# Attention forward and backward: all transposes of the probability and score-gradient slabs through the DMA crossbar, none on TensorE

## The chip, the cores and the metric

The kernel runs on one core of a Trainium2 chip. The time is device microseconds of that core, median over executions. A gain is told as a ratio: the mean time of one kernel's fast runs over the mean of the other kernel's fast runs of the same rounds on the same chip, so it is not quite the ratio of the medians that are quoted.

Engine names are those of the profile: PE is TensorE (PEld its weight loads), DVE is VectorE, ACT is ScalarE, POOL is GpSimd, SP is SyncE, whose queue issues the DMA transposes. L458 is line 458 of the kernel before; the changed kernel has the same line numbers.

## The reference, cut to what matters

The reference computes a block and all its gradients. Only the attention part is touched by the change:

```python
def _A_ref(x, k_cache, v_cache, wq, wo):
    B, Sq, D = x.shape            # 1, 2048, 576
    H, Dh = 32, 128               # 32 heads of 128; 2048 keys
    q = (x @ wq).reshape(B, Sq, H, Dh).transpose(0, 2, 1, 3)
    scores = einsum("bhqd,bhkd->bhqk", q, k_cache) * (Dh ** -0.5)
    p = softmax(scores, axis=-1)
    o = einsum("bhqk,bhkd->bhqd", p, v_cache)
    return o.transpose(0, 2, 1, 3).reshape(B, Sq, H * Dh) @ wo
# ... the whole: x + s * silu(gated MLP); outputs: the result and vjp gradients
```

For a head, the backward pass needs dV = P^T dO, dP = dO V^T, dS = P * (dP - delta), dQ = dS K and dK = dS^T Q. P and dS are 2048 x 2048 a head. They are held as 16 "slabs" of 128 rows. O = P V and dQ = dS K need each slab transposed: the kernel hands the transposed tile to these matmuls as `lhsT`.

## The kernel before: the parts that matter

A head has two phases. Phase 1 makes the scores, softmax, P slabs, O and half of dV. Phase 2 makes dP, dS slabs (written over the P slabs), dQ, the rest of dV and half of dK. The other half of dK comes in the next head's phase 1. Each slab is transposed in one of two ways:

```python
pe_p = set(cfg.get("pe_p", [0, 1, 3, 4, 6, 7, 9, 10, 12, 13, 15]))   # P slabs on TensorE: 11 of 16
pe_ds = set(cfg.get("pe_ds", [2, 5, 8, 11, 14]))                     # dS slabs on TensorE: 5 of 16
dma_p = lambda qt: qt not in pe_p
dma_ds = lambda qt: qt not in pe_ds
# ...
def transpose_slab(hs, qt, use_dma, name, engs):
    Pq = hs.slabs[qt]
    T = wpt.tile([P, NT, P], bf, name=name, tag="PT")        # 9 buffers
    if use_dma:
        nc.sync.dma_start_transpose(T[:], Pq[:])             # L452, SP queue
    else:
        for gi, g in enumerate(range(0, NT, 8)):             # the kernel's n = min(8, NT - g) is written as 8
            pt = acc_tile(bf)                                # PSUM
            for j in range(8):
                nc.tensor.transpose(pt[:, j, :], Pq[:, (g + j) * P:(g + j + 1) * P], ident[:])   # L458
            alt.copy(T[:, g:g + 8, :], pt[:, :8, :], eng=engs[gi % len(engs)])                  # L40/L42
    return T
```

A schedule gives each slab a "main" step (scores or dP and their elementwise work), a "trans" step and a "tail" step. The tail is the 16 matmuls that read the transposed slab: L500 for O, L539 for dQ. A DMA transpose is issued at the main step and used five steps later. A TensorE transpose is issued one step after main and used one step later still:

```python
SKEW_DMA = cfg.get("skew_dma", 5)
SKEW_PE = cfg.get("skew_pe", 1)
PE_TSKEW = cfg.get("pe_tskew", 1)
t_tr = qt + (0 if d else PE_TSKEW)
t_tail = t_tr + (SKEW_DMA if d else SKEW_PE)
```

## Time and profile before

| | before |
|---|---|
| time, median of 2 | 6170.7 us |
| attention stage | about 825 to 4552 us |
| head period (mean, from the second head on) | 116.3 us |
| phase 1 / phase 2 | 63.4 / 53.0 us |
| moved by DMA, a head | 12.8 MB, 110 GB/s |

The head period and the phases are differences of start times in the trace: the first weight load of a head's scores (L470) and of its dP (L523).

First the windows view. Each line is a stretch, its length, the busy time of the engines (with instructions), the granted TensorE clock, the DMA share and GB/s. The first line is the whole attention stage; the next two are phase 1 and phase 2 of one typical head.

```profile
825.00:4552.00 3727.00, 3509.97 (x46957) 2849.17 (x46955) 3144.78 (x6748) 2572.65 (x4256) 767.03 (x1305) 1.00 0.58 109
...
3609.30:3672.70 63.40, 61.66 (x845) 50.90 (x845) 56.50 (x146) 46.38 (x87) 12.78 (x26) 1.00 0.40 91
3672.70:3725.60 52.90, 48.11 (x631) 38.27 (x629) 41.87 (x68) 33.81 (x47) 11.41 (x15) 1.00 0.72 134
```

PE is busy 94% of the stage, DVE 84%, ACT 69%. Phase 1 is the fuller one on PE and the emptier one on DMA (0.40). It has 11 of its slabs on TensorE.

"Busy" overstates a pipelined engine. From start to start, a 128-column matmul takes 56 ns and a 512-column one 215 ns, while one lasts 219 and 377 ns. Counted by starts, a head holds 102.8 us of TensorE issue; the other 13.5 us of its 116.3 are stalls. The Trainium skill, "Perfetto Trace Analysis", opening note, says the same: matmul busy time "is a bad metric, because matmuls are pipelined". This trace agrees: 94% busy against 88% by starts.

Next, the page's costliest groups (busy time and mean ns after the bar, then idle time before them): the transposes on TensorE and most of their copies.

```profile
L458 PE MATMUL acct<-ident,Pq 128*128 128x128 bf16 x8192 | 591.0, 219 | 4.5 <-ACT Pq L484 4.2
...
L42 DVE COPY PT<-acct 128x1024 bf16<-128x1024 bf16 x704 | 462.7, 683 | 33.4 <-PE acct L458 30.2
```

8192 transposes at 56 ns are 459 us, or 14.3 us a head.

What PE waited for in the steady part (1000 to 4100 us): total us, times, longest.

```profile
PE dp L523 <- ACT t L529: 50.9, 188, 0.7
PE dp L523 <- DVE Pq L526: 44.6, 27, 2.0
PE sp L470 <- DVE sneg L473: 31.3, 131, 0.6
```

All three are waits for a PSUM tile that ACT or DVE still reads. There is no wait on a DMA. (The three sum to 4.8 us a head, of 13.5 us of stalls: the view counts a wait from the modelled end of the matmul before, so it shows only part of a stall.) Last, the view by tile, for PT and then for dST: the issues on the SP queue (min/median/max ns of an issue) and the time from issue to landing.

```profile
L452 SPq DMA_TRANSPOSE PT<-Pq x160: 1317/1877/3521, 840.1 to 4489.3; - x160
...
DMA to landing us min/median/max: 4.2/4.4/7.2
...
L452 SPq DMA_TRANSPOSE dST<-Pq x352: 1317/2032/8565, 889.2 to 4540.4; - x176
...
DMA to landing us min/median/max: 4.2/5.4/11.5
```

### The profile page before, as it was taken

Reading aid. Unit: us, or ns where it says so; the run is one execution under the profiler, and the core shown is the slowest. Engines: PE = TensorE matmul, PEld = TensorE weight load, DVE = VectorE, ACT = ScalarE, POOL = GpSimd, SP = SyncE. Lnnn points to the kernel's source line nnn. Section 1 sums busy time; section 2 is a strip of 40 time slices with the busy share of each in tenths; the row PEclk is TensorE's granted clock in tenths of the full one; section 3 lists DMA queues with packets and bytes.
Section 4 is the critical chain, followed back from the end, with each engine's and each line's share of the span. In section 5 each row is a group of like instructions: output and inputs, shape, how many; then the busy total and the mean of one; then the engine's idle time right before and its main releaser. Section 6 shows DMA issues by size and latency. Waiting matters only on the chain. (4 is left out here: it accounts for less than half of the span.)

```text
span 6168.1 us, 148816 instructions
## 1 busy us (share of the span) xinstructions
PE 5789.1 (94%) x63412; PEld 4164.7 (68%) x63412; DVE 3869.6 (63%) x8403; ACT 3122.5 (51%) x5420; POOL 1231.0 (20%) x2016
## 2 busy tenths in 40 slices
PE   9999989999999999999999999999978999989899
PEld 4444457777777777777777777777755677754454
DVE  5533368888888888888888888888843333311111
ACT  6412257767766766766766766766632222210000
POOL 2223111221221221221221221221211222211000
PEclk9999999999999999999999999999989999999999
DMA  7484346556556556556556556556484665594775
GB/s 276 182 203 140 130 110 117 98 114 118 100 114 114 104 114 111 106 112 114 104 110 118 104 108 120 104 105 124 91 185 142 179 183 161 173 241 143 162 147 115
DMA packets 1654747, 832.08 MB, mean 135 GB/s; under 512 B 1450352, under 2 KB 1574384, under 8 KB 1647936
## 3 DMA queue, kind: packets, MB, share of 16 engines
q1 hardware_dynamic: 1565408, 479.55, 41.2%
q0 software_dynamic: 88672, 343.01, 17.0%
q8 instruction: 495, 8.11, 0.5%
q14 instruction: 172, 1.41, 0.1%
HBM read 225.97 MB, written 234.55 MB: 75 GB/s over the span
## 5 line engine op out<-in xcount | busy, mean ns | idle before, releaser
L473 DVE TENSOR_SCALAR_CACHE_REDUCE sneg<-sp 128x1024 f32<-128x1024 f32 x1024 | 1236.9, 1216 | 76.8 <-ACT Pq L484 63.4
L484 ACT ACTIVATE Pq<-sneg,negm 128x1024 bf16<-128x1024 f32 x1024 | 1171.6, 1147 | 198.1 <-DVE negm L477 193.8
L567 PEld LDWEIGHTS <-Pq 128*128 128x128 bf16 x16384 | 1005.7, 98 | 158.8 <-issue 1.1
L529 ACT ACTIVATE t<-dp,negdelta 128x1024 bf16<-128x1024 f32 x512 | 572.4, 1118 | 350.2 <-PE dp L523 287.9
L526 DVE SCALAR_TENSOR_TENSOR Pq<-dp,delta,Pq 128x1024 bf16<-128x1024 f32 x512 | 655.1, 1279 | 96.4 <-PE acc L567 79.9
L523 PE MATMUL dp<-VT,QD 128*128 128x512 bf16 x2048 | 570.5, 378 | 151.8 <-ACT t L529 60.3
L470 PE MATMUL sp<-KT,QD 128*128 128x512 bf16 x2048 | 614.4, 378 | 56.9 <-DVE sneg L473 40.4
L458 PE MATMUL acct<-ident,Pq 128*128 128x128 bf16 x8192 | 591.0, 219 | 4.5 <-ACT Pq L484 4.2
L567 PE MATMUL acc<-Qn,Pq 128*128 128x128 bf16 x8192 | 590.5, 219 | 0.0
L567 PE MATMUL acc<-dOn,Pq 128*128 128x128 bf16 x8192 | 578.3, 219 | 0.0
L539 PE MATMUL acc<-Kn,dST 128*128 128x128 bf16 x8192 | 571.6, 219 | 3.6
L500 PE MATMUL acc<-Vn,PT 128*128 128x128 bf16 x8192 | 572.7, 219 | 0.2 <-ACT Qn L40 0.2
L458 PEld LDWEIGHTS <-Pq 128*128 128x128 bf16 x8192 | 502.6, 98 | 78.9 <-ACT Pq L484 6.9
L500 PEld LDWEIGHTS <-PT 128*128 128x128 bf16 x8192 | 499.1, 98 | 77.3 <-issue 1.3
L539 PEld LDWEIGHTS <-dST 128*128 128x128 bf16 x8192 | 495.4, 98 | 76.8 <-ACT dST L40 8.9
L530 DVE TENSOR_TENSOR Pq<-t,Pq 128x1024 bf16<-128x1024 bf16 x512 | 422.8, 826 | 143.3 <-ACT t L529 139.4
L491 POOL TENSOR_SCALAR dOn<-dOn,rinv_all 128x128 bf16<-128x128 bf16 x512 | 315.8, 617 | 862.8 <-DVE rinv_all L490 853.2
L42 DVE COPY PT<-acct 128x1024 bf16<-128x1024 bf16 x704 | 462.7, 683 | 33.4 <-PE acct L458 30.2
L523 PEld LDWEIGHTS <-QD 128*128 128x128 bf16 x2048 | 193.0, 97 | 296.0 <-issue 221.5
L506 POOL TENSOR_SCALAR negdelta<-delta 128x1 f32<-128x1 f32 x512 | 160.2, 313 | 1033.5 <-DVE rinv_all L490 579.7
L796 PEld LDWEIGHTS <-xn_all 128*128 128x128 bf16 (+1 forms) x2880 | 281.5, 100 | 40.3 <-issue 11.1
L470 PEld LDWEIGHTS <-QD 128*128 128x128 bf16 x2048 | 189.8, 97 | 160.0 <-issue 104.8
(1073 smaller groups left out, 8676.2 us busy)
## 6 DMA issues: line engine op xcount, KB each, us to landing
QD<-qd_d POOLq DMA_DIRECT2D x32, 1024.0 KB, 6.3
h_d<-h_row POOLq DMA_DIRECT2D x48, 384.0 KB, 2.7
a_d<-a_row POOLq DMA_DIRECT2D x48, 384.0 KB, 2.6
b_d<-b_row POOLq DMA_DIRECT2D x48, 384.0 KB, 3.2
a_blk<-a_d SPq DMA_DIRECT2D x18, 1024.0 KB, 5.7
h_blk<-h_d POOLq DMA_DIRECT2D x18, 1024.0 KB, 12.5
b_blk<-b_d SPq DMA_DIRECT2D x18, 1024.0 KB, 21.1
du_d<-du_blk POOLq DMA_DIRECT2D x18, 1024.0 KB, 8.5
```

Of the source, the lines that this page charges most:

```text
L42: self.nc.vector.tensor_copy(out, in_)
L458: nc.tensor.transpose(pt[:, j, :], Pq[:, (g + j) * P:(g + j + 1) * P], ident[:])
L470: nc.tensor.matmul(sp[:, c * CH:(c + 1) * CH], lhsT=hs.QT[:, qs], rhs=hs.KT[:, hf * HW_ + c * CH: hf * HW_ + (c + 1) * CH], start=True, st ...
L473: nc.vector.tensor_scalar(sneg[:], sp[:], -SCALE, None, op0=ALU.mult, op1=ALU.min, accum_out=nm[:, hf:hf + 1])
L484: nc.scalar.activation(Pq[:, hf * HW_:(hf + 1) * HW_], snegs[hf][:], AF.Exp, bias=negm[:, 0:1], scale=-1.0, accum_out=rsp[:, hf:hf + 1])
L500: nc.tensor.matmul(op_[:, 0, :], lhsT=PT[:, kt, :], rhs=hs.Vn[:, kt, :], start=(kt == 0), stop=(kt == NT - 1))
L523: nc.tensor.matmul(dp[:, c * CH:(c + 1) * CH], lhsT=hs.dOT[:, qs], rhs=hs.VT[:, hf * HW_ + c * CH: hf * HW_ + (c + 1) * CH], start=True, s ...
L526: nc.vector.scalar_tensor_tensor(Pq[:, hsl], dp[:], hs.delta[:, qt:qt + 1], Pq[:, hsl], op0=ALU.subtract, op1=ALU.mult)
L529: nc.scalar.activation(t[:], dp[:], AF.Identity, bias=hs.negdelta[:, qt:qt + 1], scale=1.0)
L530: nc.vector.tensor_tensor(Pq[:, hsl], t[:], Pq[:, hsl], op=ALU.mult)
L539: nc.tensor.matmul(qp[:, 0, :], lhsT=dST[:, kt, :], rhs=hs.Kn[:, kt, :], start=(kt == 0), stop=(kt == NT - 1))
L567: nc.tensor.matmul(self.tile[:, j, :], lhsT=self.slabs[qt][:, kt * P:(kt + 1) * P], rhs=self.rhs[:, qt, :], start=(qt == self.lo), stop=(q ...
```

## The change

The intent is to take the transposes off the engine that is the bound. All 32 slabs of a head go through the crossbar:

```diff
-    pe_p = set(cfg.get("pe_p", [0, 1, 3, 4, 6, 7, 9, 10, 12, 13, 15]))
-    pe_ds = set(cfg.get("pe_ds", [2, 5, 8, 11, 14]))
+    pe_p = set()
+    pe_ds=set()
```

The tails of those slabs also move: every tail is now five steps behind its main step.

## The prediction

> **What bounds the kernel now.** The attention stage (scores to dK/dV, 32 heads) runs from about 830 to 4560 us, 3730 of 6168 us; the change touches nothing else. In that stretch the windows view gives PE 3513 us busy (94%), DVE 3144 (84%), ACT 2569 (69%), DMA share 0.58. The head period, from the start times of the first score matmul of each head, is 116.3 us: about 63 us in phase 1 (scores, softmax, P transposes) and 53 us in phase 2 (dP, dS transposes). The waits view shows PE waiting on other engines for only about 150 us in 3400. So TensorE in order is the bound. From start to start a 128-column matmul takes 56 ns and a 512-column one 215 ns (trace), so a head has about 103 us of pure PE issue and about 13 us of small stalls.
>
> **Removed.** 16 of 32 slabs per head go through TensorE: 8192 transposes (line 458), 459 us at 56 ns, 14.3 us a head, all on the critical engine. With them go 864 DVE copies of 683 ns (590 us) and 160 ACT copies of 1.01 us (162 us), off the critical path. PE's own work falls to about 88.5 us a head, DVE to 80.
>
> **Added.** 512 more crossbar transposes of 512 KB on the SP queue, 32 a head instead of 16. Each is 2080 packets; in bins where only that queue moves data and is saturated it moves about 212 GB/s, 2.5 us per slab; issue to landing is 4.4 us undisturbed. The Trainium skill, "DMA: Bandwidth & Descriptors", section "Latency and other measured facts", states 261 GB/s with a non-contiguous middle dimension; this trace shows less, and 212 is used. Ordinary traffic is 4.1 MB a head, about 15 us. My estimate of the DMA floor: 32 x 2.5 + 15 = 95 us a head, above PE's 88.5. The bound moves from TensorE to DMA.
>
> **By phase.** Phase 2 already carries 11 transposes and about 3 MB of loads and stores; with 16 it needs about 50 to 55 us of DMA, so it gains nearly nothing. Phase 1 goes from 5 to 16 transposes (40 us plus about 1 MB) and loses 11 slabs of PE work (9.9 us): 63 to about 50 to 54 us. Where a 512 KB ordinary transfer meets a transpose, landings now come 6.5 us apart instead of 2.6; the five-step lead between transpose and use (about 16 us) then runs thin, and in-order PE stalls. I take 108.5 us a head, against 116.3: 7.8 x 32 = 250 us less.
>
> **Predicted: 5925 us (4% faster), 8 in 10 between 5740 and 6260.** Faster by over 2%: 0.70; within 2%: 0.20; slower by over 2%: 0.10.
>
> **What would show it.** PE matmuls 8192 fewer, L458 and the copies into PT and dST gone; attention PE busy falling under 90%, DMA share rising to 0.9 or more; new PE waits at L500 and L539 (the tails) released by DMA PT<-Pq and dST<-Pq; SP issues with longer durations (backpressure) and median landing of PT and dST rising from 4.4/5.4 to 7 us or more; phase 1 shortened by about 10 us, phase 2 unchanged; stages before 830 us and the last 1600 us unchanged.
>
> **What would make it wrong.** If overlapping transposes and stores slow each other beyond the mix seen here (over 3.3 us a slab), DMA needs 120 us a head and the change loses; the hand-picked split suggests that its author saw such a limit. If transposes stay at 2.3 us and PE rarely waits, a head is near 100 us and the time near 5650. A latency loop (score, softmax, transpose, tail) longer than five steps would show as PE idle with DMA not full.

## More of the kernel before

In phase 2 the two halves of a dP slab are consumed in different ways. The first goes through ACT (`t`, L529) and a DVE product (L530); the second through one DVE instruction (L526). Both free the PSUM tile `dp`, of which there are two (shared with the scores `sp`):

```python
def main2(hs, qt):
    # ... for each half hf, at high priority: dp = ps_big.tile(...); two 512-column matmuls   L523
    if stt_half(qt, hf):     # the last half
        nc.vector.scalar_tensor_tensor(Pq[:, hsl], dp[:], hs.delta[:, qt:qt + 1], Pq[:, hsl], ...)   # L526
    else:
        t = wt.tile([P, HW_], bf, name="t")
        nc.scalar.activation(t[:], dp[:], AF.Identity, bias=hs.negdelta[:, qt:qt + 1], scale=1.0)    # L529
        nc.vector.tensor_tensor(Pq[:, hsl], t[:], Pq[:, hsl], op=ALU.mult)                           # L530
```

## The result, and the profile after

The changed kernel takes 5803.0 us (5798.0 and 5808.0), ratio 0.940, 95% interval 0.938 to 0.943. That is 6% faster, inside the predicted range and 2% below the predicted 5925.

| | before | after |
|---|---|---|
| head period | 116.3 us | 105.2 us |
| phase 1 / phase 2 | 63.4 / 53.0 us | 53.4 / 51.8 us |
| TensorE issue / stalls, a head | 102.8 / 13.5 us | 88.5 / 16.7 us |
| DMA, a head | 12.8 MB, 110 GB/s | 21.2 MB, 201 GB/s |
| outside attention | 2441 us | 2437 us |

32 heads at 11.17 us each (11.2 rounded) are 357 of the 362 us between the two profiled runs, so nearly all of the gain is in the head period. The windows view after, in the same order: the stage, then phase 1 and phase 2 of a typical head.

```profile
827.00:4196.00 3369.00, 3039.31 (x38203) 2414.78 (x38773) 2683.47 (x5884) 2394.51 (x4097) 780.08 (x1306) 0.98 1.16 200
...
2295.00:2349.00 54.00, 49.34 (x633) 39.52 (x644) 45.29 (x122) 43.26 (x83) 12.34 (x24) 1.00 1.13 207
2349.00:2400.40 51.40, 44.64 (x570) 35.30 (x575) 38.64 (x64) 31.65 (x48) 12.28 (x17) 1.00 1.17 196
```

PE is busy 90% of the stage, no longer 94%. (Some 840 matmul records are missing from this trace; the stalls above are counted from the weight loads, which are all there.) The DMA share has doubled to 1.16. It adds up the times of all packets, which overlap when they queue, so it can pass 1. Both phases now move about 200 GB/s. The PE waits of the same 1000 to 4100 us, then the weight loads' largest new wait:

```profile
PE dp L523 <- ACT t L529: 109.0, 413, 0.8
PE dp L523 <- DVE Pq L526: 57.7, 29, 2.0
PE acc L539 <- DMA dST<-Pq: 46.7, 43, 5.1
PE sp L470 <- DVE sneg L473: 28.1, 77, 3.9
...
PE acc L500 <- DMA PT<-Pq: 0.7, 2, 0.4
...
PEld L539 <- DMA dST<-Pq: 55.2, 47, 5.2
```

There is a new wait on the DMA: the dQ tails wait for dST, 46.7 us on the matmuls and 55.2 us on their weight loads over 29 heads. Taken one by one in the trace, they stand at the fifth and sixth score step of the next head, where the last dS slabs of a head are used. The larger waits are still for ACT and DVE. By tile:

```profile
L452 SPq DMA_TRANSPOSE PT<-Pq x512: 1317/2618/7257, 837.5 to 4138.8; - x171
...
DMA to landing us min/median/max: 4.2/5.5/13.1
...
L452 SPq DMA_TRANSPOSE dST<-Pq x512: 1342/2887/16098, 885.3 to 4189.0; - x171
...
DMA to landing us min/median/max: 4.3/5.9/20.1
```

The issues take longer (median 2.6 and 2.9 us for 1.9 and 2.0); with half the transposes left out (e1 below) they are back at 1.9 and 2.0, so they follow the load. The median landings grow little (5.5 and 5.9 us for 4.4 and 5.4), but the longest nearly double (13.1 and 20.1 us for 7.2 and 11.5).

The result does not yet say what bounds the kernel now. The profile allows two readings. Either DMA is full and sets the pace; or TensorE with its ACT and DVE waits sets it, and the queue merely looks full because it is spread over the whole head.

### The profile page after: what moved, and what is told of

It is laid out like the page before. It is cut to its first block, busy times and chain, and to the rows that moved or that the text cites. A ratio compares the mean times of both kernels' runs of the same rounds, so it can differ in the third digit from the quotient of the medians.

```text
span 5806.2 us, 131698 instructions
## 1 busy us (share of the span) xinstructions
PE 5300.8 (91%) x54383; PEld 3729.9 (64%) x55220; DVE 3408.7 (59%) x7539; ACT 2943.8 (51%) x5260; POOL 1242.5 (21%) x2016
## 5 line engine op out<-in xcount | busy, mean ns | idle before, releaser
L567 PEld LDWEIGHTS <-Pq 128*128 128x128 bf16 x16384 | 1021.5, 98 | 219.1 <-issue 1.3
L526 DVE SCALAR_TENSOR_TENSOR Pq<-dp,delta,Pq 128x1024 bf16<-128x1024 f32 x512 | 655.7, 1281 | 112.4 <-PE acc L567 79.9
L523 PE MATMUL dp<-VT,QD 128*128 128x512 bf16 x1793 | 519.2, 384 | 193.1 <-ACT t L529 117.8
L539 PE MATMUL acc<-Kn,dST 128*128 128x128 bf16 x8192 | 577.8, 221 | 54.4 <-DMA dST<-Pq 50.1
L567 PE MATMUL acc<-Qn,Pq 128*128 128x128 bf16 x8192 | 603.2, 220 | 6.7
L500 PE MATMUL acc<-Vn,PT 128*128 128x128 bf16 x8192 | 599.6, 222 | 10.4 <-DMA PT<-Pq 5.1
L470 PE MATMUL sp<-KT,QD 128*128 128x512 bf16 x1731 | 549.5, 381 | 54.7 <-DVE sneg L473 36.0
L500 PEld LDWEIGHTS <-PT 128*128 128x128 bf16 x8192 | 519.9, 100 | 113.9 <-issue 9.9
L539 PEld LDWEIGHTS <-dST 128*128 128x128 bf16 x8192 | 501.5, 99 | 125.4 <-DMA dST<-Pq 59.1
L530 DVE TENSOR_TENSOR Pq<-t,Pq 128x1024 bf16<-128x1024 bf16 x512 | 453.9, 887 | 105.8 <-PE acc L567 53.3
L523 PEld LDWEIGHTS <-QD 128*128 128x128 bf16 x2048 | 196.9, 98 | 338.4 <-issue 253.0
L506 POOL TENSOR_SCALAR negdelta<-delta 128x1 f32<-128x1 f32 x512 | 181.9, 355 | 570.1 <-DVE junk L504 316.3
L470 PEld LDWEIGHTS <-QD 128*128 128x128 bf16 x2048 | 187.0, 97 | 141.1 <-issue 80.1
L504 DVE SCALAR_TENSOR_TENSOR junk<-acc,dOn 128x128 f32<-128x128 f32 x512 | 146.8, 289 | 102.3 <-issue 25.9
L484 ACT ACTIVATION_READ_ACCUMULATOR Pq<-sneg,negm 128x1 f32 x1024 | 203.9, 199 | 0.0
## 6 DMA issues: line engine op xcount, KB each, us to landing
b_blk<-b_d SPq DMA_DIRECT2D x18, 1024.0 KB, 21.1
```

Of the source, the lines that this page charges most:

```text
L470: nc.tensor.matmul(sp[:, c * CH:(c + 1) * CH], lhsT=hs.QT[:, qs], rhs=hs.KT[:, hf * HW_ + c * CH: hf * HW_ + (c + 1) * CH], start=True, st ...
L484: nc.scalar.activation(Pq[:, hf * HW_:(hf + 1) * HW_], snegs[hf][:], AF.Exp, bias=negm[:, 0:1], scale=-1.0, accum_out=rsp[:, hf:hf + 1])
L500: nc.tensor.matmul(op_[:, 0, :], lhsT=PT[:, kt, :], rhs=hs.Vn[:, kt, :], start=(kt == 0), stop=(kt == NT - 1))
L523: nc.tensor.matmul(dp[:, c * CH:(c + 1) * CH], lhsT=hs.dOT[:, qs], rhs=hs.VT[:, hf * HW_ + c * CH: hf * HW_ + (c + 1) * CH], start=True, s ...
L539: nc.tensor.matmul(qp[:, 0, :], lhsT=dST[:, kt, :], rhs=hs.Kn[:, kt, :], start=(kt == 0), stop=(kt == NT - 1))
L567: nc.tensor.matmul(self.tile[:, j, :], lhsT=self.slabs[qt][:, kt * P:(kt + 1) * P], rhs=self.rhs[:, qt, :], start=(qt == self.lo), stop=(q ...
```

## The experiments

Twelve kernels ran. The first four shared one chip and the other eight another, each beside runs of the kernel before. Kernels whose result is wrong on purpose are marked. "Issue" is TensorE's work by start times.

| run | DMA a head | GB/s | phase 1 / 2, us | head, us | time, us | ratio to before |
|---|---|---|---|---|---|---|
| before | 12.8 MB | 110 | 63.4 / 53.0 | 116.3 | 6170.7 | 1 |
| after | 21.2 MB | 201 | 53.4 / 51.8 | 105.2 | 5803.0 | 0.940 |
| e1 half the DMA transposes (wrong) | 12.8 MB | 124 | 51.7 / 51.6 | 103.3 | 5747.7 | 0.932 |
| e2 dead TensorE transposes and copies | 21.2 MB | 185 | 61.9 / 52.7 | 114.6 | 6123.5 | 0.993 |
| e3 dead transposes, no copies | 21.2 MB | 178 | 57.4 / 61.8 | 119.2 | 6258.4 | 1.014 |
| e4 four slabs back on TensorE | 19.1 MB | 178 | 54.9 / 52.0 | 107.0 | 5868.0 | 0.951 |
| e6 lead of 7 steps | 21.2 MB | 202 | 53.2 / 51.7 | 104.9 | 5817.1 | 0.943 |
| e7 lead of 4 steps | 21.2 MB | 199 | 54.4 / 51.9 | 106.3 | 5843.5 | 0.946 |
| e9 no t (wrong) | 21.2 MB | 203 | 60.1 / 44.1 | 104.3 | 5786.9 | 0.937 |
| e10 half more DMA transposes | 29.6 MB | 200 | 80.1 / 67.6 | 147.7 | 7166.3 | 1.162 |
| e13 half tails (wrong) | 21.1 MB | 198 | 60.7 / 45.9 | 106.7 | 5837.0 | 0.946 |
| e14 half tails, half DMA (wrong) | 12.7 MB | 136 | 49.4 / 44.3 | 93.7 | 5444.5 | 0.882 |
| e15 no t, half DMA (wrong) | 12.8 MB | 133 | 55.2 / 41.0 | 96.1 | 5520.7 | 0.895 |
| e16 dV started earlier | 21.2 MB | 201 | 52.6 / 52.8 | 105.3 | 5814.0 | 0.941 |

### First group: is DMA the bound?

**e1: every second DMA transpose left out.** Odd slabs use the transposed tile of the slab before.

```diff
         def trans1(hs, qt):
+            if qt % 2 == 1:
+                hs.PT[qt] = hs.PTprev
+                return
             hs.PT[qt] = transpose_slab(hs, qt, dma_p(qt), "PT", cfg.get("p_evac", "vv"))
+            hs.PTprev = hs.PT[qt]
# ... the same in trans2 for dST
```

> The changed kernel with every second DMA transpose left out (odd slabs reuse the transposed tile before them; the result is wrong on purpose); TensorE does none. DMA work falls to about 16 x 2.5 + 15 = 55 us a head, everything else stays. Theory (DMA is the bound after the change, at 105 us a head): TensorE's 88.5 us plus stalls of 9 to 13 us bound it, 98 to 101 us a head, so 5580 to 5680 us. Rival (the order of TensorE and the ACT/DVE steps bounds it, and the queue is full only because it is in step): within 1% of 5803 us.

Measured 5747.7 us: 1.9 us a head, a quarter to a half of what the theory promised, and within the rival's 1%. The windows of a typical head, phase 1 and phase 2:

```profile
2470.10:2521.80 51.70, 49.66 (x633) 39.69 (x644) 45.33 (x122) 43.03 (x83) 12.34 (x24) 1.00 0.63 131
2521.80:2573.20 51.40, 44.66 (x570) 35.33 (x575) 38.65 (x64) 31.62 (x48) 12.30 (x17) 1.00 0.61 117
```

The DMA share fell from 1.16 to about 0.62 and the phases hardly moved. TensorE's stalls fell from 16.7 to 14.8 us a head: the waits on dST went, and the waits on ACT and DVE stayed. So DMA cannot be the only thing that holds 105 us.

**e2: the DMA does all the work, and TensorE's transposes and their copies stay as dead work.**

```diff
+        def extra_pe(hs, qt, engs):
+            X = wx.tile([P, NT, P], bf, name="X", tag="X") if True else None
+            for gi, g in enumerate(range(0, NT, 8)):
+                pt = acc_tile(bf)
+                for j in range(8):
+                    nc.tensor.transpose(pt[:, j, :], hs.slabs[qt][:, (g + j) * P:(g + j + 1) * P], ident[:])
+                if True:
+                    alt.copy(X[:, g:g + 8, :], pt[:], eng=engs[gi])
# ... called one step after main for the slabs that were on TensorE before
-            tc.tile_pool(name="wpt", bufs=cfg.get("pt_bufs", 9)) as wpt, \
+            tc.tile_pool(name="wpt", bufs=cfg.get("pt_bufs", 8)) as wpt, \
```

> All slabs by DMA, but the 16 TensorE transposes a head and their PSUM copies stay as dead work (one transposed-tile buffer less, 8 for 9, to make room). Theory (relief of TensorE is the gain and the added DMA fits under it): 116 us a head stays, the added transposes cost 0 to 4 us a head in new waits: 6170 to 6300 us. Rival (the gain came from elsewhere, e.g. another order of the instructions): well under 6100 us.

Measured 6123.5 us, 0.8% under the kernel before and 320 us over the changed kernel. Doubling the DMA transposes alone costs nothing while TensorE needs 103 us of issue; it even saves 47 us, which the theory did not have (its range began at 6170; the rival's was "well under 6100"). So by this run no more than some 47 of the change's 368 us come without relief; the rest is the work taken off TensorE, DVE and ACT together, not a new order by itself.

**e3: the same without the copies.**

```diff
-                if True:
+                if False:
                     alt.copy(X[:, g:g + 8, :], pt[:], eng=engs[gi])
# ... against e2; no tile X, and the 9 buffers of PT kept
```

> As the run with dead transposes and copies, but without the copies: only TensorE's 14.3 us a head are put back. Theory (copies were off the critical path): at most 2% under the run with the copies, 6080 to 6280 us. Rival (relief of DVE and ACT gave a good part of the gain): 5950 us or less.

Measured 6258.4 us: within its range, but 135 us slower than e2 though it does less. Phase 2 grew to 61.8 us; some 5 us of that are 84 matmuls a head which start in phase 1 in e2 and in phase 2 here (counted by weight loads). The trace shows one new wait of about 3 us a head, TensorE's tails on a DVE instruction (77 us in 26 heads), so the two kernels differ in the order of their instructions too. They also differ in one buffer. This run therefore does not separate TensorE's share from that of the copies, and that question stays open.

**e4: four slabs back on TensorE.**

```diff
-    pe_p = set()
-    pe_ds=set()
+    pe_p = {5, 11}
+    pe_ds = {5, 11}
```

> 4 of the 32 slabs a head (2 in each phase) go back to TensorE. Theory (DMA bound): DMA loses 4 x 2.5 = 10 us a head or more, TensorE gains 3.6 to 92 us; a head falls to 99 to 102 us, 5600 to 5720 us. Rival (TensorE and its order bound): 4 x 0.9 us a head more, 5850 to 5950 us.

Measured 5868.0 us: slower, as the rival had it. TensorE's issue is 92.1 us a head and its stalls 15.0, together the 107 us of the head. DMA moved only 178 GB/s. With 28 slabs on DMA, TensorE bounds.

After this group "DMA alone is the bound" had fallen. The new theory was that TensorE with its stalls bounds, and DMA adds about 2 us of waits.

### Second group: is TensorE the bound, and DMA only a latency?

**e6 and e7: another lead between transpose and tail.**

```diff
-        SKEW_DMA = cfg.get("skew_dma", 5)
+        SKEW_DMA = cfg.get("skew_dma", 7)      # e7: 4
```

> The changed kernel with a lead of seven steps instead of five between a DMA transpose and the matmuls that use it. After the run with half the DMA transposes, the theory is: TensorE's own 88.5 us plus stalls still bounds a head, and the DMA adds about 2 us of waits a head (matmuls on dST). A longer lead takes those waits away: 5740 to 5780 us, the time of the half-DMA run. Rival (DMA throughput bounds, and the half-DMA run met another limit just below it): within 0.3% of 5803 us.

> The same with a lead of four steps. Latency theory: the waits of TensorE on PT and dST grow by 2 to 6 us a head: 5860 to 6000 us. DMA-throughput rival: within 0.5% of 5803 us.

A longer lead gained nothing (5817.1 us, where the theory had 5740 to 5780); the waits on dST only moved to other steps. A shorter lead lost 0.6% in the ratio (0.946 for 0.940), less than the latency theory's least and a little more than the rival's most. Nor did the mechanism of the latency theory show: in e7 TensorE's waits on dST did not grow, they fell. Over 1000 to 4100 us e7 has

```profile
PE acc L539 <- DMA dST<-Pq: 11.2, 13, 2.2
...
ACT nat L502 <- DMA dq_d<-nat: 92.4, 26, 7.0
```

against 46.7 us and 9.1 us in the changed kernel. The second line is ACT waiting until the store of the head before's dQ has landed. Less waiting on one DMA, more on another: if the DMA were only late, two more steps of lead should have cured it. This speaks for throughput, as the rival had it.

**e9: less work for ACT and DVE in phase 2.** The first half of each slab keeps P, so the PSUM tile is free at once.

```diff
-                else:
+                elif False:
                     t = wt.tile([P, HW_], bf, name="t")
```

> The changed kernel without the ACT step t and the DVE product for the first half of each slab in phase 2 (those columns keep P; the result is wrong on purpose). TensorE and DMA work are unchanged; ACT loses 17.9 us and DVE 14 us a head. Theory (what is left of stalls is mostly TensorE waiting for a PSUM buffer that ACT or DVE still reads): 3 to 6 us a head less, 5610 to 5710 us. DMA-throughput rival: within 0.5% of 5803 us.

Measured 5786.9 us, 0.3% off: the theory missed, and the rival's 0.5% held. But the phases tell more than the sum. Here is a typical head, phase 1 and phase 2:

```profile
2363.00:2421.90 58.90, 54.60 (x706) 44.47 (x714) 44.67 (x121) 46.45 (x87) 12.34 (x24) 0.97 1.15 205
2421.90:2467.80 45.90, 41.72 (x504) 32.40 (x506) 25.99 (x49) 12.51 (x27) 9.82 (x17) 0.96 1.21 200
```

Over all heads phase 2 fell by 7.7 us and phase 1 grew by 6.7. Some 4 us of both is only a shift of the line between them: by the weight loads, 71 of a head's 128-column matmuls now start in phase 1 instead of phase 2. The rest is in the stalls (a phase less its TensorE issue): in phase 2 they fell from 9.7 to 5.7 us, as they should when PSUM comes free sooner, and in phase 1 they rose from 7.0 to 10.0. The waits name what took the gain back; this line had 46.7 us in the changed kernel:

```profile
PE acc L539 <- DMA dST<-Pq: 184.2, 132, 7.1
```

The rate of the DMA is the same 200 to 205 GB/s in both phases.

**e10: half more DMA transposes.** After each one, a dead transpose of half a slab.

```diff
                 nc.sync.dma_start_transpose(T[:], Pq[:])
+                X = wx.tile([P, NT // 2, P], bf, name="X", tag="X")
+                nc.sync.dma_start_transpose(X[:], Pq[:, :S // 2])
# ... 8 buffers of PT for 9
```

> The changed kernel with a dead DMA transpose of half a slab after each one: 48 slabs' worth a head instead of 32 (8 transposed-tile buffers instead of 9). It measures how near the queue is to its limit. If my prediction's cost holds (2.5 us a slab plus 15 us of other traffic), DMA needs 135 us a head and the kernel takes 6700 to 6850 us. If slabs stream faster than that (2.0 us), DMA needs 111 us: 5950 to 6100 us. If DMA is far from its limit: within 2% of 5803 us.

Measured 7166.3 us, 147.7 us a head: above every range that was stated. Now TensorE waits for almost nothing else (1000 to 4100 us; the edit adds lines, so L500 and L539 are L503 and L542 here):

```profile
PEld L503 <- DMA PT<-Pq: 513.5, 276, 4.8
PEld L542 <- DMA dST<-Pq: 394.4, 164, 11.3
...
PE acc L503 <- DMA PT<-Pq: 450.1, 264, 4.6
PE acc L542 <- DMA dST<-Pq: 358.9, 160, 11.1
```

29.6 MB in 147.7 us are 200 GB/s. The changed kernel moves 21.2 MB at 201 GB/s; e6, e9 and e10 move 202, 203 and 200. For this mix of traffic the rate is a ceiling. It also does not depend on the number of issues: e10 has 64 of them a head, half of them of half size, and the rate is the same. At 200 GB/s, 21.2 MB take 106 us. The changed kernel stands on that ceiling.

It is not a ceiling of the DMA engines for any traffic. From 42 to 67 us, where only ordinary transfers run, the kernel before moves twice as much:

```profile
42.00:67.00 25.00, 25.00 (x128) 11.73 (x127) 16.50 (x47) 24.77 (x41) 6.46 (x12) 1.00 1.03 414
```

In the changed kernel 16.8 of the 21.2 MB a head are crossbar transposes, in packets of 256 bytes and from one queue, whose issues fill 97% of a head's time (33% before, 95% in e10). Whether the crossbar, the small packets or the single queue sets the 200 GB/s, no run separates.

So a third theory: two limits meet. DMA, at this mix, needs about 105 us a head, and TensorE with its stalls about 103.

### Third group: take away one limit, then both

**e13: half tails.** The tails read half of each transposed slab, so TensorE loses 14.3 us of issue a head while the DMA stream stays.

```diff
-            for kt in range(NT):
-                nc.tensor.matmul(op_[:, 0, :], lhsT=PT[:, kt, :], rhs=hs.Vn[:, kt, :], start=(kt == 0), stop=(kt == NT - 1))
+            for kt in range(NT // 2):
+                nc.tensor.matmul(op_[:, 0, :], lhsT=PT[:, kt, :], rhs=hs.Vn[:, kt, :], start=(kt == 0), stop=(kt == NT // 2 - 1))
# ... the same in tail2 for dST
```

> The changed kernel whose tails use only half of each transposed slab (8 of 16 matmuls for each output; the result is wrong on purpose). The DMA stream is unchanged; TensorE loses 14.3 us a head. Theory (two limits meet: DMA moves 21.2 MB a head at 200 to 203 GB/s, 104 to 106 us; TensorE with its stalls 103 us): the DMA holds a head at 102 to 105 us, 5720 to 5800 us. Rival (TensorE and its order bound alone, DMA never): TensorE's 14.3 us come off, at most a part lost to ACT/DVE, 5350 to 5550 us.

**e14: half tails and half the DMA transposes**, the edits of e13 and e1 together.

> As the run with half tails, but with every second DMA transpose left out too. Both theories: TensorE's relief shows once DMA is out of the way, 88 to 96 us a head, 5270 to 5520 us. If it stays above 5650 us, ACT/DVE bound it and the run with half tails says nothing of DMA.

e13 takes 5837.0 us. Taking 14 us of work a head off TensorE gains nothing; the time is even 0.6% above the changed kernel's, just over the theory's range. e14 takes 5444.5 us, 393 us less and within its range. The PE waits of e13 over 1000 to 4100 us name what held it:

```profile
PE acc L539 <- DMA dST<-Pq: 218.0, 134, 10.5
PE acc L500 <- DMA PT<-Pq: 120.9, 84, 4.2
PE sp L470 <- DVE sneg L473: 76.2, 139, 0.7
PE dp L523 <- ACT t L529: 67.6, 258, 1.0
```

The granted clock in e13's attention stage is 0.91, against 0.98 after. The less TensorE is busy in these runs, the lower the clock: busy 90% of the stage after, 81% in e13 and 71% in e10. The Trainium skill, "TensorE: Matmul & The Clock Gate", part 1 ("The HAM clock gate"), says that the gate follows how busy the engine has been; e13 (0.91) and e10 (0.88) agree. It is not what holds e13: 74.1 us of issue at 0.91 of the clock are an estimated 81 us of a head of 106.7.

**e15: no t and half the DMA transposes**, the edits of e9 and e1 together.

> As the run without t, but with every second DMA transpose left out. Without t alone phase 2 fell from 51.8 to 44.1 us and phase 1 rose from 53.4 to 60.1. Theory (DMA took it back): with half the DMA phase 1 is again 51 to 53 us and phase 2 about 44, so 95 to 98 us a head, 5490 to 5590 us. Rival (phase 1 was longer for another reason): 5690 us or more, only the 55 us that half the DMA gave before.

It takes 5520.7 us, within the theory's range. What e9 had given back was the DMA's: with half the transposes the head falls to 96.1 us, about 8 less than in e9, where the same relief gave 1.9 in e1. A typical head, phase 1 and phase 2:

```profile
2254.80:2310.00 55.20, 53.15 (x706) 43.48 (x714) 44.58 (x121) 46.14 (x87) 12.34 (x24) 1.00 0.72 130
2310.00:2350.90 40.90, 40.34 (x503) 31.50 (x504) 25.78 (x48) 12.50 (x27) 9.82 (x17) 1.00 0.66 137
```

PE is busy 96% and 99% of the phases, and TensorE's stalls are 7.7 us a head for e1's 14.8. Phase 1 stayed at 55.2 us, above the 51 to 53 that were expected, and phase 2 went below 44: the 71 matmuls (4 us) that e9 had moved across the line are in phase 1 here too, and the expectation had left them out.

Together these runs make two squares, in us a head:

| | all DMA transposes | half of them |
|---|---|---|
| the changed kernel | 105.2 | 103.3 |
| less work for ACT and DVE (e9, e15) | 104.3 | 96.1 |
| less work for TensorE (e13, e14) | 106.7 | 93.7 |

Along the column of all DMA transposes nothing helps by more than 1 us. Along the first row, relief of the DMA helps little. Only both together help. The two limits stand within 2 us of each other.

**e16: an attempt at a faster version.** At the start of phase 2, DVE waits to overwrite the P slabs until the last matmuls of dV have read them, and TensorE then stalls about 2 us once a head (L523 on DVE Pq L526 above: 57.7 us in 29 waits). Issuing that part of dV faster should end this:

```diff
-                    dvA.emit(GPI)
+                    dvA.emit(GPI + 1)
```

> A real version: the changed kernel with the first half of dV issued at 3 column blocks a step instead of 2, so that the first dS products do not wait for its last reads of the slabs (2.2 us a head of TensorE stall at the start of phase 2). Two-limits theory: DMA at 104 us a head holds the time, 5770 to 5810 us. Rival (TensorE alone bounds): 1.5 to 2.2 us a head less, 5730 to 5755 us.

Measured 5814.0 us, ratio 0.941 (0.940 to 0.943): no gain, and just over the theory's range. The stall did not go but came later and grew (85.8 us in 29 waits), so the edit did not do what it was made for and the run tests neither theory; the DMA rate stayed at 201 GB/s. No run beat the changed kernel with a right result.

## Why the prediction was right or wrong

- **The time.** Predicted 5925 us with 5740 to 6260; measured 5803. Direction, range and rough size were right. A head was put at 108.5 us and measured 105.2.
- **"TensorE in order is the bound."** Right for the kernel before. Its issue fell from 102.8 to 88.5 us a head, as costed, and 11.2 of those 14.3 us reached the time. About 3.2 came back as stalls. Some 1.9 of them go when half the DMA goes (e1).
- **"Copies off the critical path."** Not settled. e3 was to test it, and was slower than e2 for a reason that was not isolated.
- **"My estimate of the DMA floor: 95 us a head."** This is the term that was mis-sized. The ceiling of this mix is 200 GB/s for all its traffic together, so 21.2 MB need about 105 us. A fit through two runs (105.2 us with 32 slabs, 147.7 with 48) gives an estimate of 2.7 us a slab and 20 us for the rest, where 2.5 and 15 were written. The prediction still came near the time because it added a margin of 13 us for collisions on top: the floor was 10 us too low and the margin made up for it, which is luck in part.
- **"The bound moves from TensorE to DMA."** Half right. DMA is a ceiling that no relief of another engine passes by more than 1 us (e9, e13). But with half the DMA the head is still 103.3 us, so TensorE with its waits for ACT and DVE is a second limit just under it.
- **The phases.** Phase 1 was put at 50 to 54 us and measured 53.4; phase 2 was put as nearly unchanged and measured 51.8 for 53.0. The sizes were right. The reason given for phase 2, that its own DMA traffic keeps it long, is not shown: e1 halves the transposes and phase 2 stays at 51.6, so TensorE with its stalls holds that length too.
- **The signs.** DMA share over 0.9 (1.16), longer issues, and a wait at L539 on dST all came. PE busy "under 90%" came out at 90%, so it just missed. A wait at L500 on PT hardly came (0.7 us). Landings of 7 us or more did not come: the medians are 5.5 and 5.9.
- **"Over 3.3 us a slab ... the change loses."** It did not come to that: 105.2 us over 32 slabs is 3.3 us each with all other traffic included.

## What to carry to other kernels

Moving work from a full engine to an idle one gains until the second is full too, so cost the receiver by the rate at which it runs full on the same mix of traffic (here 200 GB/s with the transposes, 414 in a stretch without them), not by the time of one transfer alone. A queue that looks full doesn't prove that it is the bound, and an experiment that relieves it without much gain doesn't prove that it isn't: when two limits stand side by side, only relief of both shows either. Look at the phases as well as the sum, for what one phase gains can be given back in the next; but count first how much work each phase holds, for it can move across the line.

## What the Trainium skill lacked or had wrong

- "DMA: Bandwidth & Descriptors", section "Latency and other measured facts", gives 261 GB/s for DMA transposes with a non-contiguous middle dimension and about 350 to 400 for contiguous ones. Here slab transposes from SBUF to SBUF with 4.2 MB of ordinary traffic a head come to 198 to 203 GB/s in all (after, e6, e9, e10, e13, e16), whatever the number of issues. The page does not state a rate for such a mix. What sets the ceiling was not found.
- "VectorE: DVE Perf Modes", section "The three transpose paths", gives 390 ns on TensorE and 1309 ns by the crossbar for 128 x 128 bf16. In this kernel back-to-back transposes on TensorE start every 56 ns, and a 16-block slab through the crossbar takes 105.2 / 32 = 3.3 us, or 0.21 us a block, other traffic included. That section gives single times only and no rates of a stream. By rate TensorE is the faster path here too, and yet the kernel without it is 6% faster, because TensorE was the full engine.
- No page gives a measure of load for crossbar transposes from SBUF to SBUF. The share of DMA time is not enough: here it was 1.16 at the ceiling and 1.14 with half more transposes, but also 1.06 at 185 GB/s in e2 (1000 to 3700 us), where TensorE set the time. The GB/s say it only against the ceiling of the same mix.
